# Pairing all PSUM banks and placing loads one by one, in a kernel with a list scheduler

## Chip, cores and metric

One NeuronCore of a Trainium2 chip (trn2). The metric is the device time of one execution in microseconds; medians are over the runs of one kernel on one chip. A ratio is the mean time of one kernel's fast runs over the mean of the other's fast runs of the same rounds, so it is not quite the ratio of the medians. "The kernel before" was timed again beside every experiment and had medians from 215.5 to 216.3 us on five occasions, so experiments of different occasions are best compared by their ratios to it.

Engines: PE is TensorE, PEld its weight loads, DVE VectorE, ACT ScalarE, POOL GpSimd, SP SyncE (here it only starts loads and stores). PSUM is the memory into which PE writes its results and from which ACT and DVE read them; the kernel uses it as eight banks. The granted clock is the share of its full speed that PE's clock was given.

## The reference

Inputs are r, k, v, w, a, b of shape (4, 8, 768, 40). A recurrence with a 40x40 state runs over 768 time steps for 32 (batch, head) pairs. Its output, as rows of 320 channels, goes through a mixer.

```python
for t in range(S):                                    # per batch and head
    y[t] = r[t] @ state
    Sa = state @ a[t]
    state = state * w[t] - outer(Sa, b[t]) + outer(v[t], k[t])
x = y as (4, 768, 320)
theta = x @ w_theta
mix = w_tok_r @ (x * cos(theta)) + w_tok_i @ (x * sin(theta))   # over the 768 steps
u = x + mix
out = u + relu(u @ w_ch)
```

The kernel cuts the 768 steps into 6 chunks of 128, which gives 24 tiles (4 batches of 6). In each tile the recurrence becomes four 128x128 masked score matrices per head (psi, phi, lamv, lamu), a few transposes and small matmuls. The mixer of a batch ("rows": 12 matmuls of 320 columns for each of 6 row blocks) can start only when all six tiles of that batch are through their sines.

## The kernel before

Every piece of work is an `Op` with an engine, an assumed cost, what it reads and writes, and a priority. A list scheduler, which runs when the program is built, puts the ops of each engine in order and chooses for each PSUM result its home, one bank or two neighbouring banks out of eight. The engines then run their queues in that fixed order. Semaphore waits are not written in the kernel: the framework draws them.

```python
BANKS = 8
DOUBLE = 4
...
            o.prio = 1000.0 * (TIMES[o.spec[0]][o.spec[1]] + OFF[o.spec[2]])
...
        def find(o):                       # a home for a new PSUM result
            n = o.new[1]
            if n == 2:                     # banks (0,1) or (2,3)
                c = [(max(bank_free[b], bank_free[b + 1]), (b, b + 1))
                     for b in range(0, DOUBLE, 2)
                     if not bank_held[b] and not bank_held[b + 1]]
                return min(c) if c else None
            c = [(bank_free[b], (b,)) for b in range(DOUBLE, BANKS) if not bank_held[b]]
            return min(c) if len(c) > o.spare else None
...
    doubles = [psum.tile([128, 2, 512], FP32, name=f"ps_d{i}") for i in range(DOUBLE // 2)]
    singles = [psum.tile([128, 512], FP32, name=f"ps_s{i}") for i in range(BANKS - DOUBLE)]
    def ps(key):
        h = plan.home[key]
        return doubles[h[0] // 2] if len(h) == 2 else singles[h[0] - DOUBLE]
...
    # scores: both banks; 64-row matmuls into bank q, one mask over both banks
            t = ps(p).rearrange("p a (g c) -> p a g c", g=G)
            for g in range(G):
                for q in range(2):
                    nc.tensor.matmul(t[:, q, g, :], lhsT=lhs[rows(q), ...], rhs=rhs[rows(q), ...], ...)
        add("DVE", kindm, i, lambda: nc.vector.tensor_tensor(out=dst..., in0=ps(p)...,
            in1=mask.to_broadcast([128, 2 * G, 128]), op=ALU.mult), 1217, [p], [dkey])
...
    # everything else: one bank, e.g. transposes and their copy out of PSUM by ACT
            add("PE", kind, i, lambda: transpose_pairs(ps(p).bitcast(BF16), srcs), ..., new=(p, 1))
            evac(eng, kinde, i, p, dst, n * 128, writes=[dkey])
...
    order = plan.order()
    for o in order:
        ...
        o.fn()                             # emits the instructions
```

Of the kernel before, what the change touches and what calls it, by code (L numbers as in the profile page):

```python
# [9 lines left out]
FP32 = mybir.dt.float32  # L10
# [10 lines left out]
FREE0 = {"PE": 800.0, "ACT": 2100.0, "DVE": 4400.0, "POOL": 3600.0, "SP": 740.0}  # L21
BANKS = 8
DOUBLE = 4
INTO64, OUTOF64 = 95.0, 120.0
SP_DEPTH = 3600.0

# [7 lines left out]
class Plan:  # L34
# [34 lines left out]
    def link(self):  # L69
        ops = self.ops  # L70
        users = {}
        for o in ops:
            o.succ = []
            o.npre = len(o.pre)
            o.start = o.end = None
            o.banks = None
            o.prio = 1000.0 * (TIMES[o.spec[0]][o.spec[1]] + OFF[o.spec[2]])
            for k in set(o.reads) | set(o.writes):
                if k[0] == "ps":
                    users.setdefault(k, set()).add(o)  # L80
        for o in ops:
            o.soft = set()
            if o.new is not None and not o.loose:
                u = users[o.new[0]]
                o.soft = {p for x in u if x is not o for p in x.pre if p not in u}
                o.soft -= set(o.pre)
            o.npre += len(o.soft)
        for o in ops:
            for p in o.pre:
                p.succ.append(o)  # L90
            for p in o.soft:
                p.succ.append(o)
        return users

    def order(self):
# [4 lines left out]
        bank_free = [0.0] * BANKS  # L100
        bank_held = [False] * BANKS
# [26 lines left out]
        def find(o):  # L128
            n = o.new[1]
            if n == 2:  # L130
                c = [(max(bank_free[b], bank_free[b + 1]), (b, b + 1))
                     for b in range(0, DOUBLE, 2)
                     if not bank_held[b] and not bank_held[b + 1]]
                return min(c) if c else None
            c = [(bank_free[b], (b,)) for b in range(DOUBLE, BANKS) if not bank_held[b]]
            return min(c) if len(c) > o.spare else None

        out = []
# [1 line left out]
        while len(out) < n:  # L140
            pick = None
            for e, lst in ready.items():
                if not lst:
                    continue
                te = free[e]
                if e == "SP":
                    te = max(te, dma - SP_DEPTH)
                cand = []
                lo = None
                for o in lst:  # L150
                    t = max(te, est0[o])
                    b = None
                    if o.new is not None:
                        f = find(o)
                        if f is None:
                            continue
                        t = max(t, f[0])
                        b = f[1]
                    if e == "PE" and o.mode != mode:
                        t = max(t, te + (INTO64 if o.mode == 64 else OUTOF64))  # L160
                    cand.append((t, o, b))
                    if lo is None or t < lo:
                        lo = t
                if lo is None:
                    continue
                best = None
                for t, o, b in cand:
                    s = o.prio + WAIT * (t - lo)
                    if e == "ACT" and o.table is not None and o.table != table:
                        s += TSWITCH  # L170
                    if best is None or (s, o.idx) < best[0]:
                        best = ((s, o.idx), t, o, b)
                if pick is None or best[1] < pick[1]:
                    pick = best
            if pick is None:
                raise RuntimeError("no bank: " + str({e: [(o.kind, o.i) for o in l] for e, l in ready.items()}))
            _, t, o, b = pick
            ready[o.eng].remove(o)
            if o.eng == "ACT" and o.table is not None and o.table != table:
                table = o.table  # L180
                t += 1283
            o.start = t
            if o.new is not None:
                o.banks = b
                home[o.new[0]] = b
                for x in b:
                    bank_held[x] = True
            if o.eng == "PE":
                mode = o.mode
                o.end = t + o.cost + o.tail  # L190
                free["PE"] = t + o.cost
            elif o.work:
                free[o.eng] = t + o.cost
                if o.eng == "SP":
                    dma = max(dma, t + 1350.0) + o.work
                    o.end = dma + 600.0
                else:
                    s = max(t + 1800.0, dma - SP_DEPTH)
                    dma = max(dma, s) + o.work
                    o.end = min(dma, s + 2.0 * o.work) + 1000.0  # L200
            else:
                o.end = t + o.cost
                free[o.eng] = o.end - OVERLAP[o.eng]
            for k in set(o.reads) | set(o.writes):
                if k[0] == "ps":
                    left[k] -= 1
                    last_use[k] = max(last_use.get(k, 0.0), o.end + 50)
                    if left[k] == 0:
                        for x in home[k]:
                            bank_held[x] = False  # L210
                            bank_free[x] = last_use[k]
            out.append(o)
            for x in o.succ:
                x.npre -= 1
                if x.npre == 0:
                    make_ready(x)
# [10 lines left out]
def tail(n):  # L227
# [1 line left out]


OFF = dict(
    ah=-14.03, ch=37.4, cs=-41.22, ea=-6.95, egd=-90.74, egt=-28.2, ekb=21.31, enu=-16.72,
    enut=-11.56, er=-13.46, eth=-25.65, eut=-58.98, ev=17.32, ewt=-9.73, ex=39.26, exp=-63.71,
    ext=-55.21, gd=7.06, gt=16.39, kb=36.69, ln=-32.13, load=-20.04, loadr=-19.62, mlu=62.71,
    mlv=10.93, mphi=44.82, mpsi=69.12, nu=-17.14, nut=12.45, nx=-78.15, oo=13.49, r=35,
    row=38.73, sin=86.83, slu=-15.77, slv=39.92, sphi=-32.67, spsi=-35.87, st=34.23, ta=1.11,
    th=36.56, tkb=-1, tr=0.69, tv=4.86, uadd=-6.95, ut=37.54, v=-26.35, wdma=123.77, wt=37.8,
    x0=-27.08, xt=21.68, y=-40.12, z=24.68)
WAIT, TSWITCH = 435.08, 606442.0
TIMES = dict(  # L240
    tile=[
        -61.22, -38.55, -36.31, -3.78, 3.05, 10.64, 15.26, 42.47, 45.62, 46.74, 54.55, 58.02,
        77.61, 85.12, 102.64, 108.62, 104.48, 129.91, 135.62, 135.6, 150.73, 158.77, 165.34,
        174.78],
    row=[
        47.97, 37.38, 30.67, 33.44, 59.07, 74.74, 77.47, 97.12, 115.85, 115.75, 105.42, 129.53,
        141.42, 164.22, 173.87, 137.03, 124.06, 133.88, 191.51, 200.6, 184.9, 268.51, 279.77,
        212.96],
    rel=[
        -48.76, 34.55, 63.09, 65.85, -76.89, 92.41, 33.44, 33.52])  # L250


@with_exitstack
def kernel(
# [116 lines left out]
    wtok = dict(r=consts.tile([128, NT, S], BF16, name="wtok_r"),  # L371
                i=consts.tile([128, NT, S], BF16, name="wtok_i"))
    wrow = dict(r=sb("wrow_r", [128, S], BF16, 2), i=sb("wrow_i", [128, S], BF16, 2))
    doubles = [psum.tile([128, 2, 512], FP32, name=f"ps_d{i}") for i in range(DOUBLE // 2)]
    singles = [psum.tile([128, 512], FP32, name=f"ps_s{i}") for i in range(BANKS - DOUBLE)]
    out_r = out.rearrange("b (n p) d -> b n p d", p=128)

    plan = Plan()

    def ps(key):  # L380
        h = plan.home[key]
        return doubles[h[0] // 2] if len(h) == 2 else singles[h[0] - DOUBLE]

    def rows(p):
        return slice(64 * p, 64 * p + 64)
# [1 line left out]
    def add(eng, kind, i, fn, cost, reads=(), writes=(), at="tile", **kw):  # L387
        return plan.add(eng, kind, i, fn, cost, tuple(reads), tuple(writes),
                        (at, i, kind), **kw)
# [23 lines left out]

    def loads(i):
        for key, dst, src in load(i):
            add("SP", "load", i,
                lambda dst=dst, src=src: nc.sync.dma_start(out=dst, in_=src),
                650, [], [key], work=1030)
        bi, ci = divmod(i, NCH)
        if ci % 2 == 0:  # L420
            rr = r[bi, :, ci * C:(ci + 2) * C, :].rearrange(
                "(c g) (t q) d -> c t g (q d)", c=2, q=8)
            s = i // 2 % 2
            for c in range(2):
                add("SP", "loadr", i,
                    lambda c=c: nc.sync.dma_start(out=raw_r[s][:, c], in_=rr[c]),
                    600, [], [("raw_r", s, c)], work=520)
# [425 lines left out]
```

## Time and profile before

Median 216.16 us of three runs (215.53 to 216.28). The profiled execution was a fourth and took 214.39 us, less than any of these three. Its page, the first two parts (busy time in us, share of the span, instructions; then busy tenths in 40 equal slices of the span, and the share of the DMA engines):

```profile
span 212.6 us, 8107 instructions
## 1 busy us (share of the span) xinstructions
PE 195.1 (92%) x3344; PEld 156.3 (74%) x3344; DVE 165.5 (78%) x252; ACT 148.6 (70%) x340; POOL 117.4 (55%) x173
## 2 busy tenths in 40 slices
PE   1686899888998999999999999999999999999993
...
DMA  7998989999799999975999899977997110011222
```

The busy time by stretch (PE, PEld, DVE, ACT and POOL busy, each with its instructions; granted clock; DMA share; GB/s):

```profile
20.00:80.00 60.00, 54.94 (x1086) 44.41 (x1086) 50.34 (x57) 49.43 (x115) 43.37 (x62) 1.00 0.97 173
80.00:200.00 120.00, 119.44 (x2033) 96.78 (x2031) 98.61 (x131) 86.72 (x199) 69.94 (x98) 1.00 0.67 133
```

From 80 us on PE is full, since rows of a finished batch always wait as filler. Before 80 us nothing is full. PE "busy" includes the time in which a matmul drains while the next has started, so I read the work from the distance between starts. The timeline of PE in the kernel before (start, duration, what) shows both the work and the cost of a mode switch:

```profile
106.00 0.30 PE L724 MATMUL ps_s<-zr,wtok_r 128*128 128x320 bf16 x1
106.14 0.30 PE L724 MATMUL ps_s<-zi,wtok_i 128*128 128x320 bf16 x1
106.37 0.40 PE L522 MATMUL ps_d<-rT,nuT 64*128 64x128 bf16 x8
106.60 0.39 PE L522 MATMUL ps_d<-rT,vT 64*128 64x128 bf16 x8
106.92 0.31 PE L724 MATMUL ps_s<-zr,wtok_r 128*128 128x320 bf16 x1
```

Matmuls of 320 columns start 0.136 us apart. From the last of them to the first 64-row score matmul it is 0.23 us, so 95 ns more; back out of 64-row mode a start comes 148 ns after the last score matmul, where it would be about 26. Over the whole trace, all distances between successive matmul starts fall into these sums (us). "Matmul work" counts each distance up to about the usual one for its width at full clock (136 ns for 320 columns, 56 for 128, about 25 for small ones); what is above it is a gap or, where the mode changes, the excess at a switch. While the clock is half, the slower matmuls therefore show as short gaps.

| kernel | first matmul at | matmul work | gaps up to 0.3 us | gaps over 0.3 us | excess at switches (count) | after the last start | span |
|---|---|---|---|---|---|---|---|
| before | 4.1 | 171.0 | 8.8 | 6.9 | 18.1 (130) | 3.6 | 212.6 |

### The profile page before, as it was taken

What the parts mean: (1) busy time and instruction counts of PE and PEld (TensorE: products, weight loads), DVE (VectorE), ACT (ScalarE), POOL (GpSimd) and SP (SyncE); (2) the same over time, 40 slices, a digit from 0 to 9 for tenths busy, and PEclk for the clock granted to TensorE, in tenths of its full rate; (3) what the DMA queues carried; (4) which work ended last, traced back from release to release, by engine and by line L of the source; (5) the groups of instructions that cost most, each with busy time, mean ns of one, the idle gap of its engine ahead of it and who ended that gap; (6) DMA issues with size and microseconds to landing.
All of it is one profiled execution on the core that took longest, in us unless ns stands there. A gap on an engine that the chain in (4) does not pass through costs nothing.

```text
span 212.6 us, 8107 instructions
## 1 busy us (share of the span) xinstructions
PE 195.1 (92%) x3344; PEld 156.3 (74%) x3344; DVE 165.5 (78%) x252; ACT 148.6 (70%) x340; POOL 117.4 (55%) x173
## 2 busy tenths in 40 slices
PE   1686899888998999999999999999999999999993
PEld 1464777776786777888878888887788887777771
DVE  7537796989889779869897889978979899744533
ACT  3375858799989969968787676599967996642101
POOL 5003358578765997857688315477667488050000
PEclk9999999999999999999999999999999999999999
DMA  7998989999799999975999899977997110011222
GB/s 118 221 191 170 178 166 175 177 181 185 148 162 194 162 166 193 190 123 111 244 161 197 163 180 178 183 133 172 183 201 145 35 34 3 0 34 71 84 96 93
DMA packets 134181, 30.82 MB, mean 145 GB/s; under 512 B 125824, under 2 KB 134144, under 8 KB 134144
## 3 DMA queue, kind: packets, MB, share of 16 engines
q1 hardware_dynamic: 131712, 27.54, 66.1%
q0 software_dynamic: 2432, 2.77, 8.8%
q8 instruction: 26, 0.43, 0.9%
q14 instruction: 11, 0.09, 0.1%
HBM read 29.13 MB, written 3.93 MB: 156 GB/s over the span
## 4 chain that ended last, share of the span: by engine, by line
PE 78%; DVE 7%; ACT 4%; issue 4%; DMA 3%; POOL 2%; SPq 1%; DVEq 0%; ACTq 0%; POOLq 0%
PE ps_s L724 19%; PE ps_s L398 13%; PE ps_d L522 11%; PE ps_s L670 9%; PE ps_s L625 4%; PE ps_s L573 3%; PE ps_s L505 3%; PE ps_s L591 2%; DVE phi L527 2%; PE ps_s L654 2%; DVE psi L527 2%; PE ps_s L772 2%; DMA raw_v<-in_v_dram 2%; PE ps_d L448 2%; PE ps_s L652 2%
## 5 line engine op out<-in xcount | busy, mean ns | idle before, releaser
L468 POOL TENSOR_TENSOR kb<-raw_kb,ex 128x320 bf16<-128x320 f32 x44 | 37.3, 863 | 32.4 <-ACT ex L460 30.9
L724 PE MATMUL ps_s<-zr,wtok_r 128*128 128x320 bf16 x144 | 40.7, 300 | 0.0
L724 PE MATMUL ps_s<-zi,wtok_i 128*128 128x320 bf16 x144 | 40.6, 299 | 0.0
L527 DVE TENSOR_TENSOR psi<-ps_d,mask_p 128x1024 bf16<-128x1024 f32 x24 | 29.3, 1220 | 7.4 <-PE ps_d L522 7.3
L527 DVE TENSOR_TENSOR lamu<-ps_d,mask_p 128x1024 bf16<-128x1024 f32 x24 | 29.3, 1220 | 4.7 <-PE ps_d L522 4.2
L527 DVE TENSOR_TENSOR lamv<-ps_d,mask_p 128x1024 bf16<-128x1024 f32 x24 | 29.1, 1218 | 3.0 <-PE ps_d L522 2.9
L527 DVE TENSOR_TENSOR phi<-ps_d,mask_n 128x1024 bf16<-128x1024 f32 x24 | 29.2, 1217 | 0.7 <-PE ps_d L522 0.6
L472 POOL TENSOR_TENSOR ah<-raw_a,ex 128x320 bf16<-128x320 f32 x22 | 19.0, 863 | 16.3 <-ACT ex L460 7.6
L706 POOL TENSOR_TENSOR zr<-cs,x 128x320 bf16<-128x320 f32 x23 | 17.8, 791 | 12.9 <-ACT cs L694 12.9
L460 ACT ACTIVATE ex<-ps_d 128x648 f32<-128x648 f32 x24 | 17.2, 716 | 7.7 <-PE ps_d L456 4.6
L734 DVE TENSOR_TENSOR u<-ps_s,x 128x320 bf16<-128x320 f32 x24 | 11.7, 489 | 11.2 <-PE ps_s L724 11.1
L401 ACT COPY uT<-ps_s 128x192 f32<-128x192 f32 x24 | 7.7, 320 | 17.1 <-PE ps_s L625 17.0
L706 POOL TENSOR_TENSOR zi<-cs,x 128x320 bf16<-128x320 f32 x23 | 17.7, 791 | 2.1 <-ACT cs L694 2.0
L522 PE MATMUL ps_d<-aT,kbT 64*128 64x128 bf16 x384 | 17.2, 222 | 1.1 <-ACT aT L401 0.5
L401 ACT COPY kbT<-ps_s 128x512 f32<-128x512 f32 x24 | 14.3, 595 | 4.6 <-PE ps_s L398 3.9
L724 PEld LDWEIGHTS <-wtok_r 128*128 128x128 bf16 x144 | 14.0, 97 | 4.5
L724 PEld LDWEIGHTS <-wtok_i 128*128 128x128 bf16 x144 | 14.0, 98 | 3.6
L398 PE MATMUL ps_s<-ident,kb 128*128 128x128 bf16 x192 | 15.4, 223 | 1.3 <-DVE kb L468 1.3
L743 DVE SCALAR_TENSOR_TENSOR oo<-ps_s,u 128x320 f32<-128x320 f32 x24 | 11.6, 486 | 5.2 <-PE ps_s L670 5.2
L522 PEld LDWEIGHTS <-kbT 64*128 64x128 bf16 x384 | 11.6, 96 | 5.2 <-issue 1.7
L654 PE MATMUL ps_s<-kb,lamu 128*128 128x40 bf16 x192 | 15.0, 180 | 0.5 <-DVE lamu L527 0.4
L652 PE MATMUL ps_s<-kb,lamv 128*128 128x40 bf16 x192 | 15.4, 180 | 0.0
(113 smaller groups left out, 556.3 us busy)
## 6 DMA issues: line engine op xcount, KB each, us to landing
raw_w<-in_w_dram SPq DMA_DIRECT2D x24, 160.0 KB, 3.8
raw_kb<-in_k_dram SPq DMA_DIRECT2D x24, 160.0 KB, 4.3
raw_kb<-in_b_dram SPq DMA_DIRECT2D x24, 160.0 KB, 4.2
raw_a<-in_a_dram SPq DMA_DIRECT2D x24, 160.0 KB, 4.1
raw_v<-in_v_dram SPq DMA_DIRECT2D x24, 160.0 KB, 3.9
raw_r<-in_r_dram SPq DMA_DIRECT2D x24, 160.0 KB, 3.5
out_dram<-oo SPq DMA_DIRECT2D x24, 160.0 KB, 2.3
wrow_r<-in_moe_w_tok_r_dram POOLq DMA_DIRECT2D x6, 192.0 KB, 4.7
```

The source lines that it names most:

```text
L398: nc.tensor.transpose(out=dst[:, c:c + 128], in_=pair(src, g), identity=ident)
L401: nc.scalar.copy(out=out.bitcast(FP32), in_=in_)
L460: add("ACT", "exp", i, lambda: nc.scalar.activation(out=ex, in_=ps(pk).rearrange("p a b -> p (a b)")[:, 512 - DM:512 + DM + 8], func=AF.Ex ...
L468: lambda j=j: (nc.vector if fast else nc.gpsimd).tensor_tensor(out=paired(kb[:, j])[:, :, :, 0:D], in0=natural(raw_kb[s4][:, j]), in1=invW ...
L472: lambda: (nc.vector if fast else nc.gpsimd).tensor_tensor(out=paired(ah)[:, :, :, 0:D], in0=natural(raw_a[s4]), in1=Wi, op=ALU.mult),
L522: nc.tensor.matmul(t[:, q, g, :], lhsT=lhs[rows(q), g * 128:(g + 1) * 128], rhs=rhs[rows(q), g * 128:(g + 1) * 128], start=True, stop=True)
L527: add("DVE", kindm, i, lambda: nc.vector.tensor_tensor(out=dst.rearrange("p a b c -> p (a b) c"), in0=ps(p).rearrange("p a (g c) -> p (a g ...
L652: nc.tensor.matmul(o, lhsT=lamv[:, p, g, :], rhs=kb[:, 0, h, 0:D], start=first, stop=False, skip_group_check=True)
L654: nc.tensor.matmul(o, lhsT=lamu[:, p, g, :], rhs=kb[:, 1, h, 0:D], start=False, stop=True, skip_group_check=True)
L670: nc.tensor.matmul(dst, lhsT=lhs[:, kt, :], rhs=rhs[:, kt, :], start=kt == 0, stop=kt == 2)
L706: nc.vector if fast else nc.gpsimd).tensor_tensor(
L724: nc.tensor.matmul(ps(pk)[:, 0:DM], lhsT=wtok[nm][:, s, j * 128:(j + 1) * 128], rhs=zs[c][:, s], start=n == 0 and c == 0, stop=n == NT - 1 ...
```

## The change

Its intent: the two-bank results (score groups, cumulative sums) should not be confined to two homes while single banks stand free, and the other way round. All eight banks become four two-bank tiles; a two-bank result takes any free pair, a one-bank result takes any free bank, that is, a half of one of these tiles. All constants of the scheduler were fitted anew, with one correction for each of the 1457 ops (`ADJ`), a bonus or malus for switching PE between 64-row and 128-row mode (`PSWITCH`), and an own priority for each kind of load.

```diff
-            o.prio = 1000.0 * (TIMES[...][...] + OFF[o.spec[2]])
+            o.prio = 1000.0 * (TIMES[...][...] + OFF[o.spec[2]] + ADJ.get(o.idx, 0.0))
@@ find @@
-                     for b in range(0, DOUBLE, 2)
+                     for b in range(0, BANKS, 2)
-            c = [(bank_free[b], (b,)) for b in range(DOUBLE, BANKS) if not bank_held[b]]
+            c = [(bank_free[b], (b,)) for b in range(BANKS) if not bank_held[b]]
@@ order @@
+                    if e == "PE" and o.mode != mode:
+                        s += PSWITCH
@@ constants: OFF, TIMES, WAIT, TSWITCH all new @@
+ADJ = {0: -6.01, 1: -47.67, 2: 2.85, ...}          # cut: 1457 entries
@@ tiles @@
-    doubles = [psum.tile([128, 2, 512], FP32, name=f"ps_d{i}") for i in range(DOUBLE // 2)]
-    singles = [psum.tile([128, 512], FP32, name=f"ps_s{i}") for i in range(BANKS - DOUBLE)]
+    doubles = [psum.tile([128, 2, 512], FP32, name=f"ps_{i}") for i in range(BANKS // 2)]
-        return doubles[h[0] // 2] if len(h) == 2 else singles[h[0] - DOUBLE]
+        d = doubles[h[0] // 2]
+        return d if len(h) == 2 else d[:, h[0] % 2, :]
@@ loads @@
-            add("SP", "load", i,
+            add("SP", "l" + key[0][4:], i,
```

## The prediction

> **What bounds the kernel.** The page shows PE 92% busy, DVE 78%, ACT 70%, POOL 55%, granted clock 1.00; PE holds 78% of the chain that ended last. Busy time by stretch: from 80 to 200 us PE is busy 119.4 of 120 us and is the bound (DVE 98.6, ACT 86.7). From 20 to 80 us PE has 54.9 of 60 us, DVE 50.3, ACT 49.4, DMA share 0.97; nothing is full.
>
> PE busy overstates the work, since ends are modelled. By start-to-start times in the timeline (320 columns 136 ns, 128 columns 56 ns, small ones 25 ns) the 3344 matmuls need 171 us. The other 34 us between first and last matmul: 18.1 at the 130 switches between 64-row score matmuls and 128-row ones, 6.9 in gaps over 0.3 us, 8.8 in small ones. 4.1 us pass before the first matmul, 3.6 after the last. 28 us of the loss fall before 80 us.
>
> The skill's "TensorEngine Tiling (Array Packing)", Key Properties, says that changing the tiling mode drains TensorE. The trace agrees: median cost 95 ns into and about 122 ns out of 64-row mode, 0.217 us a pair; 65 pairs make 14.1 us, the rest of the 18.1 is waiting for data.
>
> **What the change does.** Same matmuls, masks, copies, 12 table loads and bytes.
> 1. Score groups and cumulative sums (120 two-bank uses, each about 0.4 us of PE and 1.22 us of DVE mask or 0.72 us of ACT exp) had two homes; now four, shared with single banks. The skill's "PSUM — Partial Sum Buffer" asks to guard by bank and quadrant; I take waits to stay per bank, so halves of a pair don't block each other. The built program has 493 waiting PE instructions against 542.
> 2. Another order on every engine. Score runs fall from 65 to 56: 9 x 0.217 = 2.0 us, all on PE.
> 3. Mixing rows start after 42.7 us of PE work instead of 46.0; the second switch to sine comes 8 ACT instructions earlier. Rows are the filler that makes PE full after 75 us, so earlier rows recover some early loss.
> 4. Loads one by one: the first k goes before the first w, which heads the chain (w, Ln, sums, exp); the start may be up to 0.6 us later.
>
> **Size.** Switches -2.0. Earlier filler, and DVE waiting less for scores (about 7 us from 20 to 80 us, half credited), together -5. Start +0.5. Tail unchanged. Sum about -6.5: span 206, time 209.
>
> **Predicted** 209.0 us, 8 in 10 between 203.5 and 214.5. Faster by over 2%: 0.74; within 2%: 0.23; slower: 0.03.
>
> **What would show it.** Matmul issue work stays 171 us. Switches 112, 15 to 16 us at them. Loss before 80 us falls from 28 to about 23 us; first row matmul at about 70 us (74.5 before). DVE idle before psi, lamv and lamu for PE falls from 14.4 us to under 9. After 80 us PE stays over 99% busy; tail the same. Busy times of ACT, DVE, POOL within 1%.
>
> **What would make it wrong.** Orders fitted to assumed durations may not fit the chip: one late operand stalls an in-order queue. Engines on halves of one pair may wait for each other. If DMA sets the early pace, only the switches count (214). If PE fills from 20 us on, 203 or less.

## The result

The changed kernel took 249.45 us (248.89 to 249.97, four runs) against 216.22 us; ratio 1.154, 95% interval 1.150 to 1.158. It gives the right result. It is 15% slower where I had predicted 3% faster.

The page of the profiled execution after the change:

```profile
span 248.2 us, 8027 instructions
## 1 busy us (share of the span) xinstructions
PE 207.9 (84%) x3344; PEld 162.4 (65%) x3344; DVE 168.2 (68%) x252; ACT 151.4 (61%) x340; POOL 118.0 (48%) x173
## 2 busy tenths in 40 slices
PE   1697888787878889899998998989888999998983
...
DMA  7999979992899925494969689989336010011212
```

and its busy time by stretch:

```profile
20.00:80.00 60.00, 48.60 (x928) 39.76 (x929) 43.24 (x47) 41.37 (x94) 36.23 (x51) 1.00 0.91 162
80.00:200.00 120.00, 107.30 (x1826) 84.76 (x1823) 87.04 (x109) 84.07 (x186) 68.96 (x97) 1.00 0.69 128
```

Every engine is less busy in both stretches, also after 80 us where PE had been full. The sums by distance between starts, beside those of the kernels that follow:

| kernel | first matmul at | matmul work | gaps up to 0.3 us | gaps over 0.3 us | excess at switches (count) | after the last start | span |
|---|---|---|---|---|---|---|---|
| before | 4.1 | 171.0 | 8.8 | 6.9 | 18.1 (130) | 3.6 | 212.6 |
| after | 5.2 | 171.2 | 17.7 | 29.1 | 21.4 (112) | 3.6 | 248.2 |
| e1 | 4.1 | 171.1 | 12.8 | 40.6 | 28.6 (130) | 3.7 | 260.9 |
| e2 | 5.0 | 171.2 | 9.9 | 8.0 | 13.5 (112) | 3.6 | 211.3 |
| e5 | 4.1 | 171.2 | 9.9 | 8.1 | 14.0 (112) | 3.6 | 210.8 |

The matmul work is the same, as it must be. The 36 us between the spans are almost all gaps: 22 us in long ones, 9 us in short ones, 3 us at switches although there are fewer of these. About 4 of the 9 us in short gaps fall in the time before the clock was full: by the trace's clock records it was full from 27.3 us here, from 14.8 us in the kernel before.

What do the gaps wait for? Some waits in the changed kernel make no sense as data flow. The waits by pair (who waited for whom: us in total, times, longest) have such lines as these:

```profile
ACT kbT L615 <- DVE x L875: 3.0, 1, 3.0
DVE x L875 <- PE ps L612: 3.0, 3, 1.2
...
DVE u L948 <- ACT th L894: 1.5, 1, 1.5
```

ACT's copy of the transposed k and b (kbT) needs nothing of DVE's x, x needs PE's readout matmuls but none of the transposes of line 612, and DVE's u needs nothing of ACT's copy of theta (th). None of these three stands in the waits of the kernel before or of e2 (below). For PE itself, its idle times over 0.15 us that ended with an ACT instruction sum to 7.1 us before, 24.1 us after and 7.1 us in e2; with a DVE instruction, to 6.1, 9.1 and 5.5 us. The timeline of the changed kernel at 28.5 us shows one such case in full (in brackets: idle time before, and what ended it):

```profile
28.30 0.61 PE L719 MATMUL ps<-ident,r 128*128 128x128 bf16 x8
...
28.49 0.44 ACT L791 ACTIVATE nu<-ps 128x320 bf16<-128x320 f32 x1
...
28.94 0.58 ACT L723 COPY rT<-ps 128x512 bf16<-128x512 bf16 x1
...
29.58 0.38 PE L612 MATMUL ps<-ident,nu 128*128 128x128 bf16 x4 [0.67 <-ACT rT L723]
...
30.00 0.58 ACT L723 COPY rT<-ps 128x512 bf16<-128x512 bf16 x1 [0.47 <-PE ps L612]
```

PE transposes r into a bank; ACT copies it out in two instructions (rT, twice). Between them PE transposes nu. In the built program r lies in bank 0 of the pair ps_0 and nu goes to bank 1 of the same pair. The transposes of nu have their input at 28.93, when ACT's nu ends. They start at 29.58, just after ACT's first copy of rT ends, although that copy reads the other bank. Then ACT's second copy waits 0.47 us until these transposes are through, although they wrote nothing that it reads. Each side waits for the other at a shared tile, not at a shared bank.

A count over the dependencies in the built programs agrees. Between instructions of different engines that use the same PSUM tile, the kernel before has 32,772, all with a bank in common. The changed kernel has 47,491 with a bank in common and 34,079 without.

### The profile page after: what moved, and what is told of

Its sections match the earlier page's. It is cut to its first block, busy times and chain, and to the rows that moved or that the text cites. A ratio compares the mean times of both kernels' runs of the same rounds, so it can differ in the third digit from the quotient of the medians.

```text
span 248.2 us, 8027 instructions
## 1 busy us (share of the span) xinstructions
PE 207.9 (84%) x3344; PEld 162.4 (65%) x3344; DVE 168.2 (68%) x252; ACT 151.4 (61%) x340; POOL 118.0 (48%) x173
## 4 chain that ended last, share of the span: by engine, by line
PE 43%; ACT 18%; DVE 7%; issue 5%; DMA 2%; SPq 0%; DVEq 0%; ACTq 0%
PE ps L938 14%; PE ps L884 7%; PE ps L612 6%; PE ps L736 4%; PE ps L839 3%; ACT cs L908 2%; DMA raw_r<-in_r_dram 2%; ACT rT L723 2%; ACT nu L791 2%; DVE oo L957 2%; PE ps L787 2%; ACT kbT L615 1%; ACT L908 1%; DVE gt L813 1%; ACT xT L615 1%
## 5 line engine op out<-in xcount | busy, mean ns | idle before, releaser
L938 PE MATMUL ps<-zr,wtok_r 128*128 128x320 bf16 x144 | 41.3, 299 | 6.4 <-ACT nu L791 1.7
L938 PE MATMUL ps<-zi,wtok_i 128*128 128x320 bf16 x144 | 41.2, 299 | 0.0
L741 DVE TENSOR_TENSOR psi<-ps,mask_p 128x1024 bf16<-128x1024 f32 x24 | 29.3, 1219 | 12.8 <-PE ps L736 8.8
L741 DVE TENSOR_TENSOR lamu<-ps,mask_p 128x1024 bf16<-128x1024 f32 x24 | 29.1, 1219 | 4.2 <-PE ps L736 3.8
L741 DVE TENSOR_TENSOR lamv<-ps,mask_p 128x1024 bf16<-128x1024 f32 x24 | 29.1, 1216 | 2.0 <-PE ps L736 1.8
L741 DVE TENSOR_TENSOR phi<-ps,mask_n 128x1024 bf16<-128x1024 f32 x24 | 29.2, 1215 | 0.7 <-PE ps L736 0.6
L615 ACT COPY kbT<-ps 128x512 f32<-128x512 f32 x24 | 14.1, 591 | 12.3 <-PE ps L938 3.4
L920 POOL TENSOR_TENSOR zi<-cs,x 128x320 bf16<-128x320 f32 x23 | 17.7, 792 | 5.7 <-ACT cs L908 4.9
L674 ACT ACTIVATE ex<-ps 128x648 f32<-128x648 f32 x24 | 17.3, 720 | 4.7 <-PE ps L670 2.9
L736 PE MATMUL ps<-aT,kbT 64*128 64x128 bf16 x384 | 16.5, 225 | 2.8 <-ACT aT L615 1.6
L612 PE MATMUL ps<-ident,kb 128*128 128x128 bf16 x192 | 15.9, 230 | 2.4 <-DVE kb L682 1.7
```

The costliest lines, as they stand in the source:

```text
L612: nc.tensor.transpose(out=dst[:, c:c + 128], in_=pair(src, g), identity=ident)
L615: nc.scalar.copy(out=out.bitcast(FP32), in_=in_)
L674: add("ACT", "exp", i, lambda: nc.scalar.activation(out=ex, in_=ps(pk).rearrange("p a b -> p (a b)")[:, 512 - DM:512 + DM + 8], func=AF.Ex ...
L736: nc.tensor.matmul(t[:, q, g, :], lhsT=lhs[rows(q), g * 128:(g + 1) * 128], rhs=rhs[rows(q), g * 128:(g + 1) * 128], start=True, stop=True)
L920: nc.vector if fast else nc.gpsimd).tensor_tensor(
L938: nc.tensor.matmul(ps(pk)[:, 0:DM], lhsT=wtok[nm][:, s, j * 128:(j + 1) * 128], rhs=zs[c][:, s], start=n == 0 and c == 0, stop=n == NT - 1 ...
```

## The experiments

Theory A: the framework draws waits per allocated tile; two results in halves of one tile are ordered against each other as if they shared memory. Theory B: the new order does not fit the chip, whose durations differ from the assumed ones. Theory C: the new placement of the loads does the harm. Later ones are named where they come.

### e1: only the tiles

The kernel before, with its order, its homes and all instructions, whose four single banks are halves of two two-bank tiles.

```diff
-    doubles = [psum.tile([128, 2, 512], FP32, name=f"ps_d{i}") for i in range(DOUBLE // 2)]
-    singles = [psum.tile([128, 512], FP32, name=f"ps_s{i}") for i in range(BANKS - DOUBLE)]
+    doubles = [psum.tile([128, 2, 512], FP32, name=f"ps_{i}") for i in range(BANKS // 2)]
-        return doubles[h[0] // 2] if len(h) == 2 else singles[h[0] - DOUBLE]
+        d = doubles[h[0] // 2]
+        return d if len(h) == 2 else d[:, h[0] % 2, :]
```

> The order, the homes and every instruction of the kernel before; only the four single banks are now halves of two two-bank tiles. Theory A (the compiler draws waits per allocated tile, so users of one half wait for users of the other): clearly slower than 216 us, 228 to 260. Theory B (the new order does not fit the chip; the tiles are harmless): 216 within 1.5 us. Theory C (the new placement of loads): 216 within 1.5 us.

Measured: 262.86 us, ratio 1.216 (1.210 to 1.222), correct; even 3 us above the range given for theory A. No order, no load and no address of a result changed, only which banks belong to one tile. B and C cannot explain this. Here all one-bank traffic sits in two shared pairs, in the changed kernel it is spread over four.

### e2: the changed kernel without the waits between halves

Order, homes, tiles and loads of the changed kernel. For each op that uses one bank only, the framework is told not to draw a wait on instructions of other engines that use only the other bank of the pair; a wait that also carries other data is kept (`o.pre` is the op's true dependencies).

```diff
+    def free_halves(o, names):
+        insts = made[o] = [nc.get_inst_by_name(n) for n in names]
+        banks = {x for k in set(o.reads) | set(o.writes) if k[0] == "ps" for x in plan.home[k]}
+        if len(banks) != 1:
+            return
+        b, = banks
+        keep = [x for p in o.pre for x in made.get(p, ())]
+        for x in insts:
+            tc.add_to_no_dep_group(f"{o.eng}{b}", x)
+        for x in insts:
+            for e in {"PE", "ACT", "DVE"} - {o.eng}:
+                tc.declare_no_dep(x, group=f"{e}{b ^ 1}", keep=keep, reason="the other bank of the pair")
...
+        n0 = len(nc.inst_names())
         o.fn()
+        free_halves(o, nc.inst_names()[n0:])
```

> The order, the homes and the tiles of the changed kernel, but the waits between users of different halves of one tile are not drawn (those that carry other data are kept). Theory A: the 33 us come back and the predicted gain appears, 204 to 213 us, time lost at PE before 80 us below 28 us. Theory B and theory C: stays at 245 to 250 us.

Measured: 213.72 us, ratio 0.9885 (0.982 to 0.995), correct. The 36 us between it and the changed kernel are gone, and PE is full again after 80 us:

```profile
20.00:80.00 60.00, 56.46 (x1078) 46.44 (x1076) 48.99 (x56) 49.45 (x113) 41.80 (x60) 0.96 1.03 181
80.00:200.00 120.00, 119.93 (x2062) 97.66 (x2061) 98.49 (x131) 87.86 (x203) 70.29 (x98) 1.00 0.67 131
```

The same passage in the timeline of e2:

```profile
25.57 0.61 PE L719 MATMUL ps<-ident,r 128*128 128x128 bf16 x8
25.76 0.44 ACT L791 ACTIVATE nu<-ps 128x320 bf16<-128x320 f32 x1 [0.17 <-PE ps L787]
26.21 1.07 ACT L723 COPY rT<-ps 128x512 bf16<-128x512 bf16 x2
...
26.25 0.40 PE L612 MATMUL ps<-ident,nu 128*128 128x128 bf16 x4
```

Now the transposes of nu start when nu is there, while ACT reads the other bank, and both copies of rT run back to back ("x2" merges them). The Trainium skill's page "PSUM — Partial Sum Buffer", in its section "PSUM bank collisions raise a hardware error", asks for guarding by bank and quadrant, with "by bank" as the simple version. e2 agrees for banks: with waits by bank alone the result is right. The time is 0.7 us outside the range that I had given, and the time that PE lost before 80 us (28.9 us, as before) is not below 28. So theory A holds for the slowdown, and the predicted gain is largely missing; this is taken up from e5 on.

### e4: control, e1 without the waits between halves

```diff
 (e1, with free_halves as in e2)
```

> Control for the means of e2: e1 with the waits between halves not drawn. Theory A: 216 within 1.5 us, as the kernel before. If it is far above 216, taking the waits away does not undo sharing, and e2 cannot be read as meant. Theory B: 216 as well.

Measured: 215.66 us, ratio 0.9988 (0.993 to 1.005). The means of e2 undoes what sharing adds, within the noise: e1 to e4 is 47 us for waits between banks that have nothing in common.

### e3: the new constants with the old split of banks

```diff
 (changed kernel; find(), doubles, singles and ps() as before)
```

> All new scheduling constants and the loads one by one, but the banks split as before: two two-bank tiles and four tiles of one bank. No shared halves. Theory A: 207 to 218 us, near the kernel before, since the constants were fitted to other banks. Theory B: above 225 us. Theory C: above 235 us, as the loads are placed by the same constants.

Measured: 225.63 us, ratio 1.046 (1.037 to 1.055), 144 mode switches. This is above what A allowed and, by 0.6 us, inside the range given for B: taken alone, this run speaks for B. No false waits are left here, but 10 us are lost against the kernel before. With other banks the scheduler makes another order from the same constants (144 switches in place of 112), and it is a worse one. That this is because the constants were fitted to the other pool of banks is my reading and not shown. The run is no measure of the order of the changed kernel, which e2 runs as it is.

### e9 and e8: which of the false waits cost

e9 frees only the waits between PE and a reader (ACT or DVE) of the other half, e8 only those between ACT and DVE.

```diff
-            for e in {"PE", "ACT", "DVE"} - {o.eng}:
+            for e in {"ACT": ("PE",), "DVE": ("PE",), "PE": ("ACT", "DVE")}[o.eng]:       # e9
+            for e in {"ACT": ("DVE",), "DVE": ("ACT",), "PE": ()}[o.eng]:                # e8
```

> Changed kernel in which only the waits between PE and a reader (ACT or DVE) of the other half are not drawn; ACT and DVE still wait for each other across halves. If the cost sits in PE and its readers: within 3 us of e2, 213 to 217 us. If readers waiting for readers matter: above 225 us.

> Counterpart of e9: in the changed kernel only the waits between ACT and DVE across halves are not drawn; those between PE and its readers stay. e9 left 3 to 4 us above e2. If the two kinds add up, this run saves only about 4 us: 243 to 248 us. If a wait of PE matters only together with one between readers: below 238 us.

Measured: e9 216.72 us, ratio 1.005 (1.002 to 1.009); e8 243.97 us, ratio 1.132 (1.127 to 1.138). From the changed kernel (1.154) e8 saves 2.2 points, some 5 us, and e9 14.9 points, some 32 us; e9 stays 1.7 points above e2. The two add up within a point. Most of the cost lies between PE and a reader of the other half; e9 lifts these waits in both directions, so which direction costs more is not shown.

### e10 and e11: a remedy without lifting any wait

Eight tiles of one bank. What used two banks in one instruction becomes two: a mask for each bank, an exp for each bank. e10 does this to the changed kernel, e11 to the kernel before, to price the split.

```diff
+    banks = [psum.tile([128, 512], FP32, name=f"ps_{i}") for i in range(BANKS)]
+        return banks[h[0]] if len(h) == 1 else [banks[x] for x in h]
...
+        def masks():
+            for q, x in enumerate(ps(p)):
+                nc.vector.tensor_tensor(out=dst[:, q], in0=x..., in1=mask.to_broadcast([128, G, 128]), op=ALU.mult)
```

> Order and homes of the changed kernel in eight tiles of one bank; what used two banks in one instruction (masks, exp) is two instructions, one for each bank. Theory A: far below 249 us: the time of e2 (213) plus what the split costs by e11, 213 to 226 us. Theory B (the order): above 240 us.

> The price of that split alone: the kernel before in eight tiles of one bank, masks and exp in two instructions. Estimate: a 1024-wide mask takes 1.22 us, 320-wide ones 0.49, so by a straight line two of 512 take about 1.35; 96 masks make 12 us more of DVE, of which up to 80 us (a third) a part shows: 217 to 224 us.

Measured: e11 217.64 us, ratio 1.009 (1.005 to 1.012); e10 214.71 us, ratio 0.994 (0.990 to 0.999); both correct. Theory A holds again by another way. The split costs DVE 5.8 us (171.3 busy in e11 against 165.5), half of my estimate, and 0.9% of the time.

### e5: the first w load before the first k load

From here on: why does e2 gain only 1.2%, where I had predicted 3.3%?

```diff
+    sp = [n for n, o in enumerate(order) if o.eng == "SP"][:2]
+    order[sp[0]], order[sp[1]] = order[sp[1]], order[sp[0]]
```

> e2 with its first two loads exchanged: the first w before the first k. If the loads' order costs the start what I predicted (up to 0.6 us; the first matmul of e2 came at 5.0 us against 4.1 before): the first matmul at about 4.2 us and a time 0.5 to 1.5 us below e2, 212.2 to 213.2, more if the fall of the granted clock to half between 18 and 25 us (e2) goes away with it. If the start is hidden by later waits: 213.7 within 0.5 us.

Measured: 212.70 us, ratio 0.9868 (0.985 to 0.988), correct. The first matmul comes at 4.1 us again (5.0 in e2). By the ratios this is 0.2% or 0.4 us below e2, and the two intervals overlap, so in time it is not told apart. The granted clock still fell to half, from 20.3 to 23.7 us.

### e6 and e7: loads in big packets

Theory D: loads set the pace before 80 us. Theory E: the engines do. The result is wrong: the same bytes are read as rows of 1280 contiguous bytes, not as runs of 160. e6 is the kernel before with this, e7 is e2 with this.

```diff
-            return ap[bi, :, ci * C:(ci + 1) * C, :].rearrange("h t d -> t h d")
+            n = ap.rearrange("b h (t e) d -> (b h t) (e d)", e=8)
+            return n[i * C:(i + 1) * C, :].rearrange("t (h d) -> t h d", d=D)
```

> Wrong results on purpose: w, k, b, a, v are read as rows of 320 contiguous floats (1280 bytes) in place of 8 runs of 160 bytes; same bytes, same tiles, an eighth of the packets; order and waits of the kernel before. Theory D (loads set the pace until 80 us, their share is 0.97): DMA share before 80 us well below 0.8 and a time of 206 to 213 us. Theory E (the engines' own chain sets the pace): DMA share falls as well, but the time stays at 216.3 within 1.5 us.

> The same loads (wrong results on purpose) in e2. Theory D: faster than e2 (213.7) by more than 4 us, and the distance to e6 grows beyond e2's distance to the kernel before (2.5 us), since the earlier rows and the freer banks now count. Theory E: 213.7 within 1.5 us.

Measured: e6 214.61 us, ratio 0.995 (0.993 to 0.998); e7 212.66 us, ratio 0.986 (0.983 to 0.989). The busy time by stretch of e6:

```profile
20.00:80.00 60.00, 55.64 (x1089) 45.38 (x1088) 49.19 (x56) 49.87 (x115) 42.29 (x61) 0.98 0.67 179
```

The last two columns are the point: the DMA share falls from 0.97 to 0.67 at the same GB/s (173 before, 179 now), and PE, DVE and ACT do not move. The Trainium skill's page "DMA: Bandwidth & Descriptors" says in "Why small descriptors are slow (HBM only)" that each packet carries a fixed cost; the trace agrees with the direction, with 26,661 packets against 134,181. But loads did not set the pace. The 0.5% that e6 gains is clear of noise, yet it is 0.9 us against the 215.5 us of the kernel before on that occasion, where theory D asked for 3 us or more (its 214.61 us lies between the two ranges, 0.2 us below that of E), and e7 is in the range for E. Theory D falls. A DMA share near 1 had looked like a limit and was none.

### e12, e13 and e14: relieving DVE, ACT and all

Wrong results, order as in e5. In e12 each mask covers half its columns; in e13 ACT's copies out of PSUM cover half their width; e14 has both, and the loads of e7.

```diff
-            out=dst.rearrange("p a b c -> p (a b) c"), in0=ps(p)...,                    # e12, e14
+            out=dst[:, :, 0:G // 2], in0=ps(p)...[:, :, 0:G // 2], ...
-            lambda: copy_words(dst, ps(psk)[:, 0:n // 2])                               # e13, e14
+            lambda: copy_words(dst[:, 0:n // 2], ps(psk)[:, 0:n // 4])
 (rT, nx and nu likewise; the rest of each target is zeroed at the start)
```

> Wrong results on purpose: e5 in which each DVE mask covers 512 of its 1024 columns (the rest of its target is set to zero at the start), which takes about 50 of DVE's 166 us away. e6 and e7 showed that loads don't set the pace before 80 us. Theory F (DVE's masks do): 207 us or less, PE work done by 80 us above 56 us (51 in e2). Theory G (a chain through PE, ACT, DVE and POOL, none of which is full): 209 to 212.5 us, PE work by 80 us 52 to 55 us.

> Wrong results on purpose: e5 in which ACT's copies out of PSUM (kbT, aT, vT, nuT, rT, nx, nu) cover half their width (the rest is set to zero at the start). By a straight line through 512 columns 595 ns and 192 columns 323 ns this takes about 20 to 25 of ACT's 149 us away. e12 took 50 us from DVE and gained 3 us, of which most in the first 20 us. If ACT sets the pace before 80 us: PE work done by 80 us above 56 us (51.7 in e5) and 206 to 209 us. If no single engine does: 210.5 to 212.7 us, PE work by 80 us 52 to 54 us.

> Wrong results on purpose: the half masks of e12, the half copies of e13 and the big packets of e7 together, order as e5. If several resources together set the early pace (each wait hides behind another): PE work by 80 us above 57 us and 202 to 207 us, more than the sum of the single gains. If what remains is the order itself (in-order queues, hops between engines): 207 to 210 us, little beyond e12's 209.6.

Measured, with PE's work in hand at 20 and 80 us (matmul starts weighted by their usual distance at full clock; one trace each):

| kernel | median us | ratio to before (interval) | work by 20 us | work by 80 us | between |
|---|---|---|---|---|---|
| before | 216.2 | 1 | 6.2 | 51.1 | 44.9 |
| e2 | 213.7 | 0.9885 (0.982 to 0.995) | 5.9 | 51.1 | 45.2 |
| e5 | 212.7 | 0.9868 (0.985 to 0.988) | 6.1 | 51.7 | 45.6 |
| e12 | 209.6 | 0.972 (0.969 to 0.974) | 7.7 | 54.2 | 46.5 |
| e13 | 209.3 | 0.968 (0.964 to 0.973) | 6.3 | 53.3 | 47.0 |
| e14 | 207.6 | 0.954 (0.949 to 0.960) | 6.8 | 53.9 | 47.1 |

Two of e14's four runs, and its profile, count as slow; its ratio uses the other two (205.66 and 206.50 us). The busy time by stretch of e5 and then of e12 shows how far DVE was relieved:

```profile
20.00:80.00 60.00, 56.25 (x1081) 46.02 (x1078) 49.49 (x57) 49.37 (x113) 42.30 (x61) 0.97 1.02 181
20.00:80.00 60.00, 55.46 (x1102) 45.40 (x1100) 33.76 (x59) 49.62 (x114) 44.66 (x63) 1.00 1.01 182
```

DVE falls from 49.5 (e5) to 33.8 of 60 us and PE gains 0.9 us of work between 20 and 80. So theory F (the masks set the pace) falls, by time and by work. e12 lies in the ranges for a chain in which no engine is full. e13's time lies between its two ranges (0.3 us above the one for "ACT sets the pace", 1.2 us below the other), and its early work is as given for "no single engine"; I read it so, with less certainty than e12. e14 came out between my two cases: its fast runs are in the range for "several together", but its work by 80 us is not above that of e12, and its gain over e5 (3.2 points) is not more than the single gains of e12 and e13 together (1.5 and 1.9 points). So it does not show that each wait hides behind another.

### e15: warming PE up

e5 with six matmuls of 512 columns on a constant before the first real one; the results are not used.

```diff
+    for _ in range(6):
+        nc.tensor.matmul(doubles[3][:, 1, :], lhsT=warm[:, 0:128], rhs=warm, start=True, stop=True)
```

> e5 with six matmuls of 512 columns on a constant tile before the first real one, results unused. In e5 the granted clock is half until 13.4 us and again from 20.3 to 23.7 us. If that costs time: clock full before 9 us and 0.5 to 2 us below e5 (212.7), so a version that beats both kernels by more. If the start is bound by waits for other engines: within 0.4 us of e5.

Measured: 212.47 us, ratio 0.985 (0.981 to 0.989), correct: not told apart from e5. The dummies ran from 1.5 us on, but the trace has the clock full from 13.0 us (13.4 in e5) and half from 19.8 to 23.2 us, as in e5. The halved clock was thus not removed, and its cost stays unmeasured. A rough estimate from the traces: 128-column transposes start 107 ns apart at half clock and 56 ns at full, so the work that PE did at half clock is about the most that it can have cost. In the step alone that is 3.2 us in e2 (18.1 to 24.9 us) and 1.5 us in e5; with the start, where the clock is half in all of them, it is 5.1 us in e2, 4.6 in e5 and 3.7 in the kernel before. The trace of the kernel before has no such step.

## Why the prediction was wrong

**The step that failed** is in point 1: "I take waits to stay per bank, so halves of a pair don't block each other." e1 shows +47 us from sharing tiles alone, e2 shows that without such waits the changed kernel takes 213.7 and not 249.5 us, e4 that the means undoes just this, and e10 the same with separate tiles. The scheduler's own model keeps books by bank, and so did I; the framework's are by tile. The list of what would make the prediction wrong named it ("engines on halves of one pair may wait for each other"), but without weight: it lay outside the range.

**The evidence that I gave for it was none.** "493 waiting PE instructions against 542" counts instructions that wait, not what they wait for. A false wait often rides on an instruction that waits anyway, with a higher count. It needed a look at whom single waits name. The same count in a rebuild of the programs (541 before, 492 after) gives 506 for e1: sharing alone makes fewer instructions wait and costs 47 us.

**"What would show it", point by point.**

| sign | predicted | after | e2 |
|---|---|---|---|
| matmul work, us | 171 | 171.2 | 171.2 |
| switches, us at them | 112, 15 to 16 | 112, 21.4 | 112, 13.5 |
| first row matmul, us | about 70 | 81.3 | 70.7 |
| PE work by 80 us (before: 51.1) | about 5 more | 41.8 | 51.1 |
| DVE idle before psi, lamv, lamu for PE (14.4) | under 9 | 14.4 | 12.5 |
| PE busy 80 to 200 us | over 99% | 89% | 99.9% |
| busy ACT, DVE, POOL (148.6, 165.5, 117.4 us) | within 1% | +1.9, +1.6, +0.5% | +0.1, +0.1, +0.4% |

**Terms of the sum, read in e2, where the false wait is gone.** Switches: predicted -2.0 us, measured -4.6 (18.1 to 13.5), as waits for data beside the drains fell too. The Trainium skill's page "TensorEngine Tiling (Array Packing)", Key Properties, has the drain but no figure; the trace has 95 and 122 ns. Start: predicted +0.5, first matmul +0.9 us. Filler and scores: predicted -5, measured 0 by 80 us. Rows did start 3.7 us earlier, as predicted, but in these two traces PE had done the same work by 80 us: the earlier rows took the place of other work and filled no gaps. DVE's waits for scores fell by 1.9 us, not by half. Gaps that are no switches grew by 2.2 us. This makes -4.6 + 0.9 + 2.2 + 0.2 (work) = -1.3, the difference of the spans. These are differences of two single traces, and that of the kernel before was a fast one (214.39 us): by the ratios e2 gains 2.5 us, of which the sum explains half. How far single traces differ shows e4, which has the order of the kernel before and, by the ratio, its time: PE work by 80 us was 48.8 us there against 51.1, and the clock was full only from 23.1 us against 14.8. The zero for filler and scores is thus uncertain by some 2 us; the predicted 5 are still not there.

**Where the rest of the expected gain is.** Before 80 us PE does about 45 us of work in 60, whatever I relieved: loads (e6, e7), DVE (e12), ACT (e13), all of them (e14) move it by 1.5 us at most against e5. More free banks did not visibly move it either (e2 against before, one trace each). Two things are left. One is the order with its hops from engine to engine in queues that do not overtake; that is argued by exclusion and not shown. The other is the granted clock: e2, e5, e7, e9, e10, e13, e14 and e15 all have a step at half clock between 18 and 25 us, as has e6, and e12, which has none, has the most work by 80 us (54.2). By the estimate under e15 the step is worth 1.5 to 3 us at most, and no run has tested it, since e15 did not remove it. The rest stays open, and so does where after 80 us e13 and e14 won the part of their time that the early work does not explain.

**A version that beats both kernels.** e5 (ratio 0.987, 212.7 us) and e15 (0.985), which are correct; with ordinary tiles e10 (0.994). All are below 2%: the change, freed of the false waits, is worth 1 to 1.5%.

## What to carry to other kernels

Find out at what grain your framework draws its waits before you let two independent results share one allocation: put two of them into one tile, build, and look whether one names the other. A scheduler that keeps its books finer than the framework plans overlaps that cannot happen. And a resource with a busy share near 1 (here the DMA engines) is a limit only if relieving it moves the time; one run with wrong data tells.

## What the Trainium skill lacked or had wrong

- No page that I read says at what grain this kernel's framework draws the waits that it generates. "PSUM — Partial Sum Buffer" gives the rule by bank and quadrant, which e2 shows to suffice by bank; that a two-bank tile used by halves can be ordered as one object, at a cost of 47 us of 216 (e1 against e4), is missing there.
- "TensorEngine Tiling (Array Packing)" says that a change of the tiling mode drains TensorE, but has no figure: 95 ns into and about 122 ns out of 64-row mode.
- "TensorE: Matmul & The Clock Gate", Part 1, lets sustained activity release the clock after about 3.4 us. Six dummy matmuls from 1.5 us on did not bring that forward (full from 13.0 us in e15, 13.4 in e5), but they ran only until about 4 us, so for less than that. The steps at half clock agree with its window: 3.4 us in e5, 6.8 us in e2. Nothing here contradicts the page. What no page has: the mean granted clock that the profile views list leaves out the time before the trace's first clock record. It is 1.00 for the kernel before, although that record comes at 14.8 us and the 128-column transposes started 107 ns apart until 13.5 us and 56 ns apart from 15.2 us.
